# Skip rows in one 512-wide operation, weight loads tied to exps, and a later bank preload in a fused SSM and attention kernel

## Chip, cores and metric

The kernel runs on one core of a Trainium2 chip. The metric is the device time of one execution in microseconds (us). Each kernel was executed several times, and the kernel before ran beside it on the same chip; medians are quoted.

## The reference, cut to what matters

```python
def reference(A_x, ..., B_wqkv, B_wo, gate_w):           # x is 1 x 2048 x 1024
    x = A_x
    g = sigmoid((x * gate_w).sum(-1, keepdims=True))
    # SSM branch: a recurrence over the 2048 positions, then
    #   a = 2 * Re(h @ C^T) + x * Dskip                    <- "x * Dskip" is the skip row
    a = A_ref(x, Lambda, B, C, log_dt, Dskip)
    # attention branch: 32 heads of 32, softmax(q k^T / sqrt(32)) v, then @ wo
    b = B_ref(x, wqkv, wo)
    return g * a + (1 - g) * b
```

## The kernel before

One stream for every engine computes both branches in 512 periods. ScalarE (ACT) does the exps of the scores, TensorE the matmuls, VectorE (DVE) evictions, the SSM scan, skip rows and some exps, and SyncE (SP) issues nearly all DMAs in order. A scheduler notes reads and writes by token and puts in the semaphore waits. These are the parts that the change and the argument touch.

```python
def ld_xn(self, ch, tq, cb):              # two loads of 128 x 256 for one skip row
    for k in range(2):
        c0 = 512 * cb + 256 * k
        self.dma(lambda e, ...: e.dma_start(self.xn[k], self.x2[..., c0:c0 + 256]), [], [("xn", k)] + over, "ld_xn")

def skip_ops(self, ch, tq, cb):           # Ag[:, 0] = xn * g * Dskip, in two halves
    for k in range(2):
        ... scalar_tensor_tensor(self.Ag[:, 0, 256 * k:256 * (k + 1)], self.xn[k], self.gcol[...], self.drow[...], mult, mult)

# SSM output tile: add the matmuls' sum to the skip row, then store the tile
def evac():
    self.dve(... scalar_tensor_tensor(a, ps[:, 7, :], self.gcol[...], a, mult, add) ..., "evac_c")
    self.dma(lambda e: e.dma_start(self.agd[tile], a), ..., "st_a")     # the next skip row overwrites a

# three weight loads of 256 KB for the group after next
for k, part in enumerate((1, 2, 0)):
    if pg == (58 + 2 * k if g else 24):   # pg is the period within its group of 64
        self.ld_w(g + 2, part)

# the tail
self.pv([(last - 1, q) for q in range(4)])
preload()                                 # four 512-wide matmuls that prepare a bank
pv(0); norm(0)                            # last value sums, first part, and their scaling
pv(1); xp(0); norm(1)
```

Every stream ends alike. A check on the results leaves a flag; each engine reads it and jumps over a fallback program to its last block (cut):

```python
def stream(name, e):
    S.emit(name, e, sems, MARK_AT[name], lambda: loc.append(e.mark_branch_hint_location()))
    ...
    e.wait_ge(sems[fast.flag_op.lane], fast.flag_op.tick)
    e.reg_load(r, flag[0:1, 0:1])
    br = e.br_cmp(r, 0, on_true="done_" + name, on_false="bad_" + name, comp_op="IS_EQ")
    br.branch_hint(loc[0])
    with e.bass.body("bad_" + name):      # fallback: 246 instructions on SyncE
        ...
    e.bass.switch_bb("done_" + name)
    if name == "sp":
        S.final_waits(e, sems, True)      # the last stores
```

## Time and profile before

| | before |
|---|---|
| time, median of 3 runs | 918.78 us |
| span of the profiled execution | 916.8 us |
| busy: TensorE, ACT, VectorE | 902.4, 902.1, 757.3 us |
| period of the one visible stall in the body | 2.83 us (others 1.8 to 1.9) |
| flag copy, and the span's end after the start of it | 914.08, 2.8 us later |

Times in a profile count from the start of the profiled execution. The body is bound by ACT (busy 902.1 of 916.8 us, and the weight loads of the score matmuls wait 82.9 us for its exps); the tail from the last exp at 909.59 on is a chain of single steps. The lines of the profile stand in the prediction.

### The profile page before, as it was taken

To read this page: it belongs to the slowest core of one execution; us is meant where nothing else is said; L and a number is where in the kernel's file an instruction comes from. 1 tells how busy PE (TensorE), PEld (TensorE's weight loads), DVE (VectorE), ACT (ScalarE), POOL (GpSimd) and SP (SyncE) were. 2 spreads that over 40 slices of the span, in tenths; PEclk is the share of its full clock that TensorE was granted. 3 is DMA by queue.
4 is the path that set the end of the run, shared out by engine and by line. 5 is a ranking of instruction groups with operands and counts; after the bars stand their busy time and mean duration, and the time that the engine had idled before them with its cause. 6 is when DMAs were issued, how large, how long until landed. Compare 5 with 4: busy or idle time off the path is not lost.

```text
span 916.8 us, 33709 instructions
## 1 busy us (share of the span) xinstructions
PE 902.4 (98%) x15196; PEld 513.6 (56%) x15196; DVE 757.3 (83%) x1394; ACT 902.1 (98%) x1034; POOL 33.4 (4%) x63
## 2 busy tenths in 40 slices
PE   8999999999999999999999999999999999999997
PEld 4556655555555655665556555556555655555554
DVE  4499998999989899998988975789999776676675
ACT  6999999999999999999999999999999999999997
POOL 0500000010000001000000010000000000000000
PEclk9999999999999999999999999999999999999999
DMA  9558631322311305222222113231330122533422
GB/s 205 108 88 129 105 59 40 54 44 57 87 39 39 72 24 86 44 51 48 62 65 31 49 62 87 66 63 31 54 63 8 52 65 70 177 88 119 123 65 75
DMA packets 166867, 65.37 MB, mean 71 GB/s; under 512 B 146880, under 2 KB 155584, under 8 KB 166720
## 3 DMA queue, kind: packets, MB, share of 16 engines
q1 hardware_dynamic: 164416, 62.52, 30.8%
q8 instruction: 120, 1.97, 0.9%
q10 hardware_dynamic: 2304, 0.67, 0.3%
q14 instruction: 27, 0.22, 0.1%
HBM read 21.24 MB, written 12.62 MB: 37 GB/s over the span
## 4 chain that ended last, share of the span: by engine, by line
PE 92%; DVE 3%; ACT 3%; DMA 1%; issue 0%; SPq 0%
PE f_ps L1853 26%; PE f_ps L1758 18%; PE f_ps L1545 12%; PE f_ps L1517 12%; PE f_ps L1485 11%; PE f_ps L1578 6%; PE f_ps L1505 5%; ACT f_cT_re L1781 1%; DVE f_tq L1423 1%; ACT f_pt L1781 1%; DMA f_xT<-in_A_x_dram 1%; ACT f_cT_im L1781 1%; ACT f_Et L1781 1%; ACT f_OT L1781 1%; DVE f_ht L1431 1%
## 5 line engine op out<-in xcount | busy, mean ns | idle before, releaser
L1781 ACT ACTIVATE f_pt<-f_ps 128x1024 bf16<-128x1024 f32 x840 | 800.5, 1156 | 1.2 <-PE f_ps L1758 0.6
L1853 PEld LDWEIGHTS f_ps<-f_V,f_pt 128*128 128x128 bf16 x6720 | 232.8, 96 | 137.1 <-issue 86.5
L1853 PE MATMUL f_ps<-f_V,f_pt 128*128 128x33 bf16 x6720 | 285.4, 178 | 0.3
L1758 PE MATMUL f_ps<-f_Q,f_K 32*128 32x256 bf16 x4096 | 213.1, 273 | 2.6 <-ACT f_cT_re L1781 1.2
L1758 PEld LDWEIGHTS f_ps<-f_Q,f_K 32*128 32x128 bf16 x4096 | 67.4, 92 | 120.9 <-ACT f_pt L1781 63.4
L1517 PE MATMUL f_ps<-f_xT,f_wb 128*128 128x512 bf16 x512 | 131.1, 377 | 1.5 <-DVE f_ub L1523 0.4
L1485 PE MATMUL f_ps<-f_xT,f_wb 128*128 128x512 bf16 x464 | 119.0, 378 | 0.3 <-DVE f_Q L1490 0.2
L1431 DVE TENSOR_TENSOR_SCAN f_ht<-f_pf,f_init,f_ut 128x512 bf16<-128x512 f32 x64 | 81.2, 1275 | 0.0
L1805 DVE TENSOR_SCALAR f_wb<-f_ps 128x512 f32<-128x512 f32 x83 | 56.8, 685 | 27.4 <-PE f_ps L1758 26.5
L1545 PE MATMUL f_ps<-f_cT_re,f_hp 128*128 128x512 bf16 x192 | 72.6, 378 | 0.9 <-DVE f_Ag L1554 0.8
L1545 PE MATMUL f_ps<-f_cT_im,f_hp 128*128 128x512 bf16 x192 | 72.5, 378 | 0.0
L1578 PE MATMUL f_ps<-f_wb,f_OT 128*128 128x512 bf16 x248 | 63.9, 378 | 0.2
L1804 ACT ACTIVATE f_wb<-f_ps 128x512 bf16<-128x512 f32 x83 | 60.8, 732 | 0.6 <-PE f_ps L1758 0.6
L1517 PEld LDWEIGHTS f_ps<-f_xT,f_wb 128*128 128x128 bf16 x512 | 40.3, 96 | 34.2 <-issue 2.2
L1505 PE MATMUL f_ps<-f_wb,f_xT 128*128 128x128 bf16 x896 | 59.1, 219 | 0.3
L1812 DVE SCALAR_TENSOR_TENSOR f_wb<-f_Ag,f_wb 128x512 int16<-128x512 f32 x83 | 56.7, 683 | 0.6
L1811 DVE SCALAR_TENSOR_TENSOR f_Ag<-f_wb,f_Ag 128x512 f32<-128x512 uint16 x83 | 56.7, 683 | 0.5
L1810 DVE SCALAR_TENSOR_TENSOR f_Ag<-f_wb 128x512 f32<-128x512 uint16 x83 | 56.6, 682 | 0.3
L1485 PEld LDWEIGHTS f_ps<-f_xT,f_wb 128*128 128x128 bf16 x464 | 36.2, 96 | 28.7 <-DVE f_Q L1490 0.3
L1505 PEld LDWEIGHTS f_ps<-f_wb,f_xT 128*128 128x128 bf16 x896 | 50.5, 97 | 0.9 <-issue 0.4
L1523 DVE CAST f_ub<-f_ps 128x512 bf16<-128x512 f32 x48 | 33.1, 690 | 14.8 <-PE f_ps L1517 14.1
L1423 DVE TENSOR_TENSOR f_tq<-f_ht,f_Et 128x1024 bf16<-128x1024 bf16 x64 | 42.8, 685 | 0.4
(158 smaller groups left out, 892.7 us busy)
## 6 DMA issues: line engine op xcount, KB each, us to landing
ag_scratch<-f_Ag SPq DMA_DIRECT2D x32, 256.0 KB, 2.0
f_hp<-ag_scratch SPq DMA_DIRECT2D x32, 256.0 KB, 3.0
f_wb<-in_B_wqkv_dram SPq DMA_DIRECT2D x21, 256.0 KB, 4.0
out_dram<-f_xT SPq DMA_DIRECT2D x14, 256.0 KB, 2.1
f_xa<-in_A_x_dram SPq DMA_DIRECT2D x32, 64.0 KB, 1.9
f_pf<-in_A_x_dram SPq DMA_DIRECT2D x32, 64.0 KB, 1.9
f_wb<-in_B_wo_dram SPq DMA_DIRECT2D x1, 1024.0 KB
f_OT<-f_On SPq DMA_TRANSPOSE x63, 2.3
```

The source lines that it names most:

```text
L1431: ops.append((1.192, lambda ri=ri: dve(lambda e: e.tensor_tensor_scan(ht[:, ri, :], rr, ut[:, ri, :], self.init[:, ri, j:j + 1], ALU.mult, ...
L1485: mms.append((1, lambda e, f, l, a=a: e.matmul(ps[:, bank, :], w[:, g % 2, part, a, :], xT[:, a, 512 * ch:512 * (ch + 1)], start=f, stop=l ...
L1505: m = e.matmul(ps[:, bank, 128 * q:128 * (q + 1)], xT[:, a, 128 * kt:128 * (kt + 1)], w[:, g % 2, 2, a, :], start=(a == 0), stop=(a == 7))
L1517: mms.append((1, lambda e, f, l, a=a: e.matmul(ps[:, 7, :], bT[:, n % 2, ri, a, :], xT[:, a, 512 * ch:512 * (ch + 1)], start=f, stop=l), [ ...
L1545: mms.append((1, lambda e, f, l, j=j, ri=ri: e.matmul(ps[:, 7, :], hp(tq, ri, j), cT[ri][:, j, 512 * cb:512 * (cb + 1)], start=f, stop=l), ...
L1578: mms.append((1, lambda e, f, l, j=j: e.matmul(ps[:, 7, :], OT[:, j, 256 * qb + 128 * r:256 * qb + 128 * (r + 1)], wo[j][0][:, 512 * cb:51 ...
L1758: m = e.matmul(ps[:, 2 * sl[z] + h % 2, 256 * kl:256 * (kl + 1)], K[32 * h:32 * h + 32, g % 2, 128 * kt:128 * (kt + 1)], Q[32 * h:32 * h + ...
L1781: self.act(lambda e: e.activation(self.tile[p], ps[:, 2 * s:2 * s + 2, :], ACT.Exp, bias=OCTAVES * LN2, scale=LN2 / 128), [("S", s)], [("p ...
L1804: self.S.op("act", lambda e: e.activation(t[:, 0, :], ps[:, 2 * s, :], ACT.Exp, bias=OCTAVES * LN2, scale=LN2 / 128), reads=[("S", s)], wr ...
L1805: self.S.op("dve", lambda e: e.tensor_scalar(xi, ps[:, 2 * s + 1, :], BITS_0, BITS_MIN, ALU.add, ALU.max), reads=[("S", s)], writes=[("xi" ...
L1811: (0.603, lambda: self.dve(lambda e: e.scalar_tensor_tensor(xw, lo, CUBE_C, xw, ALU.add, ALU.mult), [I, W], [W], "exp_c")),
L1853: m = e.matmul(ps[:, 6, o:o + 33], self.tile[p][:, h2, 256 * kl + 128 * qt:256 * kl + 128 * (qt + 1)], V[:, g % 2, 2 * i + kl, h, :], star ...
```

## The change

Its intent: halve the number of skip-row instructions and loads, space the three weight loads so that they don't crowd a store, and let the last bank preload fill a time in which TensorE waits. The diff, cut to its core (the buffers of the skip rows are joined to match; three runs of the dense order move):

```diff
-DVB_RUNS = (... (502, 506))
+DVB_RUNS = (... (502, 506), (509, 509))          # one more exp half on VectorE
 ...
     def act(self, fn, r, w, name=""):
-        return self.S.op("act", ...)
+        self.last_act = self.S.op("act", ...)
+        return self.last_act
 ...
     def ld_w(self, g, part, eng="sp"):
-        deps = []
+        deps = [self.last_act] if g > 1 else []
 ...
-        for k in range(2):                           # ld_xn
-            self.dma(... self.xn[k] <- 256 columns ...)
+        self.dma(... self.xn <- 512 columns ...)
 ...
-            ops.append((0.335, ... 256 columns ...)) # skip_ops, twice
+        ops = [(0.665, ... 512 columns ...)]
 ...
         self.pv([(last - 1, q) for q in range(4)])
-        preload()
         pv(0)
         norm(0)
+        preload()
         pv(1)
 ...
-    MARK_AT = dict(pe=100, act=260, dve=115, sp=900)
+    MARK_AT = dict(pe=100, act=260, dve=279, sp=900)
```

The last line moves the place of VectorE's branch hint.

## The prediction

> **What bounds the kernel now.** The kernel computes a state-space branch (SSM) and a 32-head attention branch in one stream of 512 periods. Each period does one block of scores on TensorE, two exps of 128x1024 scores on ScalarE (ACT), the value sums (PV) of an older block, and about four 512-wide "dense" matmuls (projections, SSM, output). In 102 of the periods half of one exp goes to VectorE (DVE) as four 512-wide instructions. I read the page first, then the groups by line, then the table of waits, then the timeline.

> ```profile
> PE 902.4 (98%) x15196; PEld 513.6 (56%) x15196; DVE 757.3 (83%) x1394; ACT 902.1 (98%) x1034; POOL 33.4 (4%) x63
> L1781 ACT ACTIVATE f_pt<-f_ps 128x1024 bf16<-128x1024 f32 x840 | 800.5, 1156 | 1.2 <-PE f_ps L1758 0.6
> ```

> Two engines show 98%. The table of waits says which of them waits for the other:

> ```profile
> PEld f_ps L1758 <- ACT f_pt L1781: 63.4, 152, 0.4
> PEld f_ps L1758 <- ACT f_wb L1804: 19.5, 46, 0.4
> DVE f_Ag L1366 <- DMA ag_scratch<-f_Ag: 1.9, 3, 1.0
> PEld f_ps L1545 <- DVE f_Ag L1554: 0.9, 1, 0.9
> ACT f_pt L1781 <- PE f_ps L1758: 0.6, 1, 0.6
> ```

> The weight loads of the score matmuls wait about 83 us for exps in the first two rows, because a bank of scores is free only when an exp has read it. ACT hardly waits for TensorE. So ACT is the bound. Its floor: one run of nine full exps starts at 883.68 and the next exp at 891.91, so a full exp costs 8.23 / 9 = 0.914 us; half exps start about 0.48 us before their successor. The groups have 922 full and 102 half exps: 922 x 0.914 + 102 x 0.48 = 892 us. The first exp starts at 9.77 and the last ends at 909.59, 900 us. Everything that better order can win between is thus about 8 us, 0.9% of the time; behind it lies a tail of 7.2 us.

> The third and fourth wait rows are the one visible stall in the body. In the timeline (start, length, what):

> ```profile
> 566.36 0.57 SPq L1100 DMA_DIRECT2D f_wb<-in_B_wqkv_dram  x1
> ...
> 568.07 0.43 SPq L1555 DMA_DIRECT2D ag_scratch<-f_Ag  x1
> 568.54 1.24 SPq L1100 DMA_DIRECT2D f_wb<-in_B_wqkv_dram  x2
> ...
> 572.47 0.48 DVE L1366 SCALAR_TENSOR_TENSOR f_Ag<-f_xa,f_gcol,f_drow 128x256 f32<-128x256 bf16 x1 [1.02 <-DMA ag_scratch<-f_Ag]
> ...
> 574.47 0.74 DVE L1554 SCALAR_TENSOR_TENSOR f_Ag<-f_ps,f_gcol,f_Ag 128x512 f32<-128x512 f32 x1
> ...
> 575.26 0.10 PEld L1545 LDWEIGHTS f_ps<-f_cT_re,f_hp 128*128 128x128 bf16 x1 [0.95 <-DVE f_Ag L1554]
> ...
> 576.89 0.60 ACT L1804 ACTIVATE f_wb<-f_ps 128x512 bf16<-128x512 f32 x1 [0.62 <-PE f_ps L1758]
> ```

> Read downward: three weight loads (256 KB each) are issued at 566.36 and 568.54, around the store of an SSM row. The store, usually landing in 2.0 us, lands only about 4.4 us after its issue, because the next skip row, which overwrites its source, starts at 572.47. The eviction of the SSM sum slips to 574.47, TensorE waits for the bank until 575.26, and ACT runs dry before 576.89. That period takes 2.83 us from score load to score load, where those without a VectorE exp usually take 1.8 to 1.9.

> [...] with a per-partition scalar, 128, 256 and 512 elements take 342, 477 and 750 ns here, so the fixed part is about 205 ns. [...]

> **The change part by part.**

> *Skip rows.* Now two operations and two 64 KB loads per row, 32 rows:

> ```profile
> L1366 DVE SCALAR_TENSOR_TENSOR f_Ag<-f_xa,f_gcol,f_drow 128x256 f32<-128x256 bf16 x32 | 15.3, 477 | 2.0 <-DMA ag_scratch<-f_Ag 1.9
> L1366 DVE SCALAR_TENSOR_TENSOR f_Ag<-f_pf,f_gcol,f_drow 128x256 f32<-128x256 bf16 x32 | 15.3, 477 | 0.0
> ```

> One 512-wide operation should take about 0.75 us (the 512-wide eviction with the same kind of scalar takes 750 ns). Summed: 32 x (2 x 0.477 - 0.75) = 6.5 us of busy time, or, since two adjacent ones start 0.40 apart and end 0.88 after the first start, 32 x 0.13 = 4.2 us of VectorE time. VectorE is 83% busy and not the bound, so nearly all of this is beside ACT. I give it 0.2 us for rows in which VectorE is late. The 32 saved loads sit on the sync queue, which waits for most of its time anyway: 0.

> *Weight loads tied to exps.* A group's three loads now wait for the latest exp of periods 58, 60 and 62 of the group before. Two periods are about 3.6 us, so by the period starts the loads at the stall should go at about 566.4 (as now), 569.2 and 572.8 instead of 566.4, 568.5 and 569.1. The store then competes with the second half of one load and the first part of another; my estimate for its landing is 2.5 to 3.3 us, that is 570.6 to 571.4. The skip row was ready at 572.47 - 1.02 = 571.45. The wait goes. The period falls from 2.83 to about 1.85: up to 0.98 us. ACT's own loss confirms the size: its exp of 574.97 should be followed at 575.88 by the one of 576.89, 1.0 us. I count 0.9. The two other waits on stores in the third row (0.7 and 0.2) cost ACT nothing visible. The weights are needed only from the next group on, over 3 us later, so lateness of the third is harmless.

> *Order of the rows.* The dense order moves three projections and SSM sums near period 250 and one near period 30. Matmul counts are unchanged. No stall stands there in the waits: 0.

> *One more VectorE exp, in period 509.* This is in the diff, not in its heading. ACT saves 0.914 - 0.48 = 0.43 us. But in the last periods TensorE and VectorE set the pace: each "rest" output row waits for the eviction of the one before.

> *Value sums ahead of the preload.* Now the chain ends so:

> ```profile
> 908.43 0.76 PE L1853 MATMUL f_ps<-f_V,f_pt 128*128 128x33 bf16 x24
> 909.04 1.02 PE L2162 MATMUL f_ps<-f_Et,f_ident 128*128 128x512 bf16 x4
> 909.90 0.36 PE L2173 MATMUL f_ps<-f_V,f_pt 128*128 128x33 bf16 x8
> 910.29 0.18 DVE L2180 RECIPROCAL f_rc<-f_ps 128x4 f32<-128x4 f32 x1 [0.91 <-PE f_ps L2173]
> 911.02 0.35 PE L2173 MATMUL f_ps<-f_V,f_pt 128*128 128x33 bf16 x8 [0.76 <-DVE f_On L2181]
> ```

> The preload (0.87 us on the chain) stands ahead of the value sums, and TensorE then idles 0.76 us behind them for the normalisation. Swapped, the preload fills that idle time: alone it would win about 0.8 us.

> Both together, in the order of the changed instruction streams: VectorE has evict, exp a (period 509), evict, exp b, exp c, evict, exp d, evict; TensorE has, behind the last scores, the eight value sums that need exp d, then a rest row, 32 value sums, the preload. From the present times: second eviction at 905.18, b 905.85, c 906.57, third eviction 907.24, d 907.91 to 908.6 (spacings of 0.67, dependent ones 0.72). TensorE stands from about 907.1 to 908.65 for exp d. Then 0.1 + 3 x 0.216 + 32 x 0.025 brings it to 910.2, and the reciprocal starts 0.19 later, 910.4 against 910.29. So the new VectorE exp eats what the preload wins: tail +0.1 us.

> *Sum.* -0.9 - 0.2 + 0.1 = -1.0 us; I add -0.2 for smaller DMA collisions at the other groups' loads. 918.8 - 1.2 = 917.6.

> **The rivals.** (1) The stall stays or moves: the store is still between two loads, or the third load now delays another transfer. For it: two periods are barely one load's 4.0 us to landing. Against: the skip row has 1 us less to bridge. Then the time is about 918.7. (2) The exp in period 509 is quicker than I reckon, or its value sums do not hold TensorE: then the 0.8 us of the preload is won in full, and 0.1 more from ACT: about 916.6. (3) VectorE's lower load lets its exps finish sooner all over the body. At most it wins part of the 8 us; for it speaks that VectorE is over 90% busy in many slices, against it that TensorE's waits for VectorE are near 1 us in sum outside the stall and normalisations. That would give about 916.

> **Range and chances.** The three known terms are each below 1 us and the three timed runs spread by 0.7 us. Rival 2 or 3 gives the low end 916.1, rival 1 with a worse tail the high end 918.8. 2% is 18 us, over twice what all order could win, and no part adds work on ACT; a failure of another kind keeps 0.01 each.

> **What will show it.** Skip rows of about 750 ns, x32. No wait of a skip row for a store near 572, no 0.95 wait of the SSM matmuls for its eviction, and a period of about 1.85 there. In the tail, a TensorE wait of over 1 us for the last VectorE exp step, and the preload between the two groups of last value sums with hardly any idle time. Were the tail 0.7 us shorter, my timing of exp d is wrong; were the body more than 2 us shorter, ACT had hidden gaps that I did not see.

## The result, and the profile after

The changed kernel took 921.58 us (median of 5 runs, 921.0 to 922.81), the kernel before 918.88 us beside it (5 runs, 918.45 to 919.49). The ratio is 1.0029, 95% interval 1.0015 to 1.0044. (A ratio is the mean time of one kernel's runs over that of the other's in the same rounds, so it is not quite the ratio of the medians.) The prediction was a gain of 1.2 us; it is a loss of 2.7 us, outside the range. All outputs are right.

The bound has not moved. From the page of the changed kernel, busy times and the costliest group:

```profile
PE 882.3 (96%) x14977; PEld 513.4 (56%) x15196; DVE 756.2 (82%) x1366; ACT 902.0 (98%) x1034; POOL 33.4 (4%) x63
L1777 ACT ACTIVATE f_pt<-f_ps 128x1024 bf16<-128x1024 f32 x839 | 799.6, 1155 | 1.3 <-PE f_ps L1754 0.6
```

ACT is as busy as before. TensorE's lower figure is no gain: the page has 14977 matmuls to 15196 weight loads, so 219 matmul records are missing from this trace.

The groups by line show the skip rows as predicted, and with them a first bad sign, the waits in the last column:

```profile
L1362 DVE SCALAR_TENSOR_TENSOR f_Ag<-f_pfx,f_gcol,f_drow 128x512 f32<-128x512 bf16 x32 | 23.9, 746 | 3.8 <-DMA ag_scratch<-f_Ag 3.6
```

They take 746 ns each, but they wait 3.6 us for stores, where the two halves waited 1.9. The timeline of the stall (start, length, what):

```profile
566.62 0.58 SPq L1101 DMA_DIRECT2D f_wb<-in_B_wqkv_dram  x1
...
567.86 0.43 SPq L1551 DMA_DIRECT2D ag_scratch<-f_Ag  x1
...
569.66 3.62 SPq L1101 DMA_DIRECT2D f_wb<-in_B_wqkv_dram  x2
...
572.95 0.75 DVE L1362 SCALAR_TENSOR_TENSOR f_Ag<-f_pfx,f_gcol,f_drow 128x512 f32<-128x512 bf16 x1 [1.23 <-DMA ag_scratch<-f_Ag]
...
575.74 0.10 PEld L1541 LDWEIGHTS f_ps<-f_cT_re,f_hp 128*128 128x128 bf16 x1 [1.16 <-DVE f_Ag L1550]
```

The loads are spaced as foreseen: 566.62, 569.66 and, as the second of the "x2", 572.90. The store between the first two nevertheless lands only 5.0 us after its issue (the view of that one transfer gives its landing), just before the skip row starts. The stall is all there, and the period is 3.04 us long.

The tail of the changed kernel, in the timeline:

```profile
909.21 0.17 PEld L1849 LDWEIGHTS f_ps<-f_V,f_ub 128*128 128x128 bf16 x4 [1.32 <-DVE f_ub L1808]
...
910.58 0.35 PE L2169 MATMUL f_ps<-f_V,f_pt 128*128 128x33 bf16 x8
...
910.97 0.18 DVE L2176 RECIPROCAL f_rc<-f_ps 128x4 f32<-128x4 f32 x1
910.99 0.81 PE L2158 MATMUL f_ps<-f_Et,f_ident 128*128 128x512 bf16 x3
...
911.69 0.35 PE L2169 MATMUL f_ps<-f_V,f_pt 128*128 128x33 bf16 x8
...
914.76 0.14 DVE L2227 CAST flag<-f_ps 1x1 int32<-1x1 f32 x1
```

TensorE waits 1.32 us for the last VectorE exp step, and the preload (910.99; one of its four matmul records is missing) fills the time between the two groups of value sums. The flag copy comes at 914.76, 0.68 us later than before; the body brought 0.64 of that to the tail. So the body and the tail explain only a quarter of the 2.7 us. The rest comes after the flag. The view by windows shows it (window, length, busy time and count of PE, PEld, DVE, ACT, POOL, then granted clock, DMA share, GB/s). First before, then after:

```profile
916.00:917.00 1.00, 0.00 (x0) 0.00 (x0) 0.00 (x0) 0.00 (x0) 0.00 (x0) 0.54 0.16 41
```

```profile
918.00:919.00 1.00, 0.00 (x0) 0.00 (x0) 0.00 (x0) 0.00 (x0) 0.00 (x0) 0.50 0.00 0
919.00:920.00 1.00, 0.00 (x0) 0.00 (x0) 0.00 (x0) 0.00 (x0) 0.00 (x0) 0.50 0.03 8
```

Before, the span ends at 916.8, inside the first line. After, there is a whole microsecond in which no engine works and nothing moves, and in the next one a few KB move. (The granted clock of the changed kernel is 1.00 in the stretches up to 915 us, 0.89 from 915 to 916 and 0.50 from there to the end; over the span that makes its mean of 0.998.) What the engines do there is not in the views, because branches and semaphore instructions aren't counted as work, but the trace has their records. I read SyncE's last ones and the instruction fetches of 8 KB from them:

```
start of                       before    after
flag copy (VectorE)            914.08    914.76
SyncE reads the flag           914.98    916.00
SyncE's branch                 915.76    916.55
SyncE's next instruction       916.29    918.98
8 KB instruction fetches       916.22    916.68
after the flag                 916.49    916.97
                               916.85    917.18
                                         919.55
end of the span                916.84    919.54
```

The next instruction of TensorE, ACT and VectorE follows their branch by 0.49 to 0.61 us before and by 0.49 to 0.62 us after. SyncE's takes 0.53 us before and 2.43 us after, and there is a fourth fetch. The flag to the end takes 2.8 us before and 4.8 us after. That is 2.0 of the 2.7 us.

### The profile page after: what moved, and what is told of

It is laid out like the page before. It is cut to its first block, busy times and chain, and to the rows that moved or that the text cites. A ratio compares the mean times of both kernels' runs of the same rounds, so it can differ in the third digit from the quotient of the medians.

```text
span 919.5 us, 33420 instructions
## 1 busy us (share of the span) xinstructions
PE 882.3 (96%) x14977; PEld 513.4 (56%) x15196; DVE 756.2 (82%) x1366; ACT 902.0 (98%) x1034; POOL 33.4 (4%) x63
## 4 chain that ended last, share of the span: by engine, by line
PE 80%; ACT 11%; DVE 4%; issue 2%; DMA 2%; SPq 1%; DVEq 0%
PE f_ps L1849 23%; PE f_ps L1754 16%; PE f_ps L1541 11%; PE f_ps L1513 11%; PE f_ps L1481 9%; ACT f_pt L1777 7%; PE f_ps L1501 5%; PE f_ps L1574 4%; DMA ag_scratch<-f_Ag 1%; SPq L1093 1%; ACT f_Et L1777 1%; ACT f_cT_re L1777 1%; DMA f_xT<-in_A_x_dram 1%; ACT f_OT L1777 1%; ACT f_cT_im L1777 1%
## 5 line engine op out<-in xcount | busy, mean ns | idle before, releaser
L1513 PE MATMUL f_ps<-f_xT,f_wb 128*128 128x512 bf16 x448 | 118.4, 377 | 8.5 <-issue 3.2
L1481 PE MATMUL f_ps<-f_xT,f_wb 128*128 128x512 bf16 x406 | 106.8, 378 | 5.6 <-issue 1.1
L1427 DVE TENSOR_TENSOR_SCAN f_ht<-f_pfx,f_init,f_ut 128x512 bf16<-128x512 f32 x64 | 81.2, 1274 | 0.0
L1541 PE MATMUL f_ps<-f_cT_im,f_hp 128*128 128x512 bf16 x180 | 68.0, 378 | 3.6 <-DVE f_Ag L1550 1.3
L1541 PE MATMUL f_ps<-f_cT_re,f_hp 128*128 128x512 bf16 x157 | 59.4, 378 | 0.8
L1574 PE MATMUL f_ps<-f_wb,f_OT 128*128 128x512 bf16 x217 | 57.5, 378 | 2.7 <-issue 0.3
```

The lines of the kernel that those rows point to most:

```text
L1427: ops.append((1.192, lambda ri=ri: dve(lambda e: e.tensor_tensor_scan(ht[:, ri, :], rr, ut[:, ri, :], self.init[:, ri, j:j + 1], ALU.mult, ...
L1481: mms.append((1, lambda e, f, l, a=a: e.matmul(ps[:, bank, :], w[:, g % 2, part, a, :], xT[:, a, 512 * ch:512 * (ch + 1)], start=f, stop=l ...
L1513: mms.append((1, lambda e, f, l, a=a: e.matmul(ps[:, 7, :], bT[:, n % 2, ri, a, :], xT[:, a, 512 * ch:512 * (ch + 1)], start=f, stop=l), [ ...
L1541: mms.append((1, lambda e, f, l, j=j, ri=ri: e.matmul(ps[:, 7, :], hp(tq, ri, j), cT[ri][:, j, 512 * cb:512 * (cb + 1)], start=f, stop=l), ...
L1574: mms.append((1, lambda e, f, l, j=j: e.matmul(ps[:, 7, :], OT[:, j, 256 * qb + 128 * r:256 * qb + 128 * (r + 1)], wo[j][0][:, 512 * cb:51 ...
```

## The experiments

Eighteen kernels ran in five batches, each beside the kernel before, whose medians were 918.62, 918.89, 918.68, 918.69 and 918.75 us. "Same" and similar words compare with those.

### The branch hint

The changed kernel with VectorE's hint back at 115, and the kernel before with it at 279. Theory H puts the late end down to the hint's new place.

```diff
-    MARK_AT = dict(pe=100, act=260, dve=279, sp=900)
+    MARK_AT = dict(pe=100, act=260, dve=115, sp=900)     # after_hint115; before_hint279 the other way
```

> The changed kernel with one number put back: VectorE's prefetch hint for the last branch stands again 115 instructions before the end of its stream instead of 279. Theory H[...]: the gap from VectorE's flag copy to the end of the span falls from 4.7 us to about 2.7 us, the fetch on the instruction queue 2.4 us behind the others vanishes, and the time is about 919.6 us. Rival S (the longer end is the landing of the last output stores, made later by the order of the tail): the gap stays 4.7 us and the time stays 921.6 us.

Measured: 921.17 us, ratio 1.0029 (1.0015 to 1.0042), with 2.51 us between SyncE's branch and its next instruction.

> The kernel before with only VectorE's prefetch hint moved from 115 to 279 instructions before the end. Theory H: the gap from the flag copy to the end grows from 2.6 to about 4.7 us and the time rises by 2.0 us to about 920.9 us. Rival S (last stores): no change, 918.9 us. A third reading, that the hint's best place depends on the instruction count of the changed kernel, also gives no change here.

Measured: 918.90 us, ratio 1.0005 (0.9991 to 1.0019), 0.53 us. The place of VectorE's hint changes nothing that these two runs can resolve.

A late hint for SyncE itself was tried later, on the changed kernel:

```diff
-    MARK_AT = dict(pe=100, act=260, dve=279, sp=900)
+    MARK_AT = dict(pe=100, act=260, dve=279, sp=60)
```

> The changed kernel with SyncE's branch hint 60 operations before its end instead of at the start of its stream. If [...]SyncE's own hint comes so early that its effect is gone by the end in the changed kernel: gap 2.8 us, time 919.3. If the hint does nothing for this branch (as the place of VectorE's did nothing for the time): gap 4.8 us, 921.3.

Measured: 921.51 us, ratio 1.0027 (1.0013 to 1.0040), 1.96 us after the branch. That doesn't mend it either.

### Where SyncE's last branch stands

The 32 loads that the change saves, and fewer waits, make SyncE's stream 40 instructions shorter. Counted in the compiled programs, its last branch stands at instruction 378 before and at 338 after; the target at 624 and 584, behind the 246 instructions of the fallback. I put instructions that do nothing back into the middle of SyncE's stream.

```diff
             if mark is not None and k == max(0, n - mark_at):
                 mark()
+            if eng_name == "sp" and pad is not None and k == 100:
+                for _ in range(40):                       # before_pad88_main: 88
+                    eng.nop().then_inc(pad, 1)            # nobody waits for it
```

> The changed kernel with 40 instructions that do nothing (they add one to a semaphore that nobody waits for) put in the middle of SyncE's stream, where it idles; so its last branch and the final block that it jumps to stand at the same places in SyncE's stream (instructions 378 and 624) as in the kernel before. Theory F (the 2.0 us at the end come from where SyncE's last branch and its target stand in the stream, 40 instructions earlier in the changed kernel[...]): the gap from the start of the flag copy to the end of the span falls from 4.8 to 2.8 us, SyncE's next instruction comes 0.45 us after its branch and not 2.35, no fetch after the flag beyond three, time 919.3 (-2.0 or so). Rival G (the late end comes from something in the data traffic or the semaphores of the changed kernel, for example fewer loads counted on the queue): the gap stays 4.8 us and the time 921.3.

Measured: 919.04 us, ratio 1.0002 (0.9989 to 1.0016). SyncE's next instruction comes 0.53 us after its branch, there are three fetches after the flag, and the span ends 2.8 us after the flag copy. This is theory F's outcome (0.53 us for the 0.45 that it expected, 919.04 for 919.3); 40 instructions of no use make the changed kernel 2.1 to 2.5 us faster.

```diff
                     if name == "sp":
                         S2.final_waits(e, sems2)
+                        for _ in range(40):               # in the fallback, never executed
+                            e.nop().then_inc(pad, 1)
```

> The changed kernel with 39 more instructions in SyncE's fallback code, which never runs and which SyncE's last branch jumps over: the branch stays where the change put it (338), its target moves from 584 to 623, the distance grows from 246 to 285. Theory F in its form 'the place of the target counts' (before: 624, 0.45 us): the gap falls to 2.8 us and the time to 919.3. Theory F in its form 'the place of the branch, or the distance, counts': the gap stays 4.8 us, the time 921.3. Rival G: stays, too; the run with 40 in the executed stream tells those two apart.

Measured: 921.10 us, ratio 1.0030 (1.0017 to 1.0044), 2.10 us after the branch, four fetches. The 40 lines add 39 instructions, so the target stands at 623, one short of its old place. Bringing only the target back doesn't help.

> The kernel before with 88 such instructions in the middle of SyncE's stream: its branch stands at 466 and the target at 712, which is 128[...] beyond the places of the changed kernel, so the same place within a fetched block. Theory F with blocks of 128: the kernel before gets the late end: gap 4.8 us, SyncE's next instruction 2.35 us after its branch, one more fetch, time 920.6 (+2.0). With blocks of 256 instead, or under rival G: gap 2.8 us and 918.7, unless the padding itself costs, which it should not, since SyncE is idle there.

Measured: 924.15 us, ratio 1.0055 (1.0042 to 1.0069). The late end came, as F says: 2.42 us after the branch, four fetches, 4.8 us from the flag to the end. But the flag was late as well, at 917.24. The trace has SyncE's 88 extra instructions from 279.76 to 285.29, and the load of a skip row behind them goes out at 285.37, where in the kernel before it went at 280.38; from 300 us on all is 3.1 us late. My assumption that SyncE was idle there was wrong for 88; later runs spread the padding over as many operations.

This run shows one thing more. The padding starts 0.06 us apart, but once there are 0.40 us between two of them: between the 208th and the 209th instruction of SyncE's stream (284.51 and 284.92), and an 8 KB fetch follows at 285.55. I call such a place an edge. Two more show below by a pause of 0.39 us, behind the 336th and the 464th instruction, so the three are 128 instructions apart. I call the 128 instructions from one edge to the next a block.

With spread padding I asked how wide the good range is, and whether it repeats (a step, in the last expectation, is the 128 instructions from one edge to the next):

```diff
+            if eng_name == "sp" and pad is not None and 100 <= k < 122:   # 22, 52; from 80 on: 92, 168
+                eng.nop().then_inc(pad, 1)
```

> The changed kernel with 22 instructions that do nothing spread over SyncE's stream: branch at 360, target at 606, halfway between the slow place (338) and the fast one (378). If only a narrow range of places is fast[...]: slow, SyncE's next instruction 2.3 us after its branch, 921.3. If the range is wide: 0.5 us, 919.3.

Measured: 919.22 us, 0.53 us after the branch.

> The changed kernel with 52 such instructions: branch at 390, target at 636, 12 beyond the fast place. Narrow range of about 10 places: slow, 2.3 us, 921.3. Wide range: 0.5 us, 919.3.

Measured: 918.43 us, 0.53 us.

> The changed kernel with 168 such instructions, one after each of 168 operations: branch at 506, target at 752, which is 128 beyond the fast place of 378. If the places repeat with the 128 instructions of an 8 KB fetch: 0.5 us, 919.3 (somewhat more if the padding delays a transfer). If they repeat with 256 or not at all: 2.3 us, 921.3.

Measured: 919.13 us, 0.53 us.

> The changed kernel with 92 instructions that do nothing, one after each of 92 operations of SyncE: branch at 430, target at 676. [...] If the good range reaches from some place between 341 and 360 to half a step further: slow, SyncE's next instruction 2.3 us after its branch, 921.2. If most places are good and only those around 338 to 350 are bad: 0.5 us, 919.2.

Measured: 919.10 us, 0.53 us. The narrow good range that I had in mind fell: 360, 390, 430 and 506 are as good as 378, and the changed kernel met a bad place. All profiled runs, by the place of the branch, with the time from SyncE's branch to its next instruction and the number of 8 KB fetches after the flag:

```
branch at               runs                                                    us          fetches
338                     after, after_hint115, after_no509, after_sp_hint_late   1.96-2.51   4
338 (target at 623)     after_pad40_fallback                                    2.10        4
340                     after_loads_late                                        2.31        4
466 (= 338 + 128)       before_pad88_main                                       2.42        4
360                     after_pad22                                             0.53        3
378                     before, before_hint279, before_swap, before_skip,
                        after_pad40_main, best_a, best_b                        0.53        3
379, 380                before_tie, best_c                                      0.53        3
390, 430                after_pad52, after_pad92                                0.53        3
506 (= 378 + 128)       after_pad168                                            0.53        3
```

No run falls between the two kinds, and the edges sort them. In every slow run the branch is the second or the fourth instruction behind an edge (337 and 465 are the first). The pause of 0.39 us shows there, too: just ahead of the read of the flag in the runs at 338 and 466, and two instructions earlier in the run at 340. Here are SyncE's last records of three runs (W a wait, R the read of the flag, B the branch, N the next instruction):

```
kernel changed, 338:    W 915.54  W 915.61  R 916.00  B 916.55                       N 918.98
loads late, 340:        W 914.69  W 915.08  W 915.17  R 915.24  B 915.76             N 918.07
before, 378:            W 914.86  W 914.92  R 914.98  B 915.76                       N 916.29
```

So in the slow runs SyncE passes an edge, and its branch starts 0.9 to 1.1 us after the last instruction ahead of that edge. In the fast ones the last edge is at least 23 instructions back. The fourth fetch after the flag fits: above, a fetch came 0.6 us behind the 209th instruction, the first after an edge, and in the slow runs such a fetch would fall behind the flag. (The last fetch of a run is not the extra one: in all profiles, fast and slow, it comes 0.55 to 0.81 us after SyncE's next instruction.) How near the target is does not sort the runs. Counted on in steps of 128, which no pause shows for the targets, the slow branch at 338 has its target (584) in the next block and all fast ones in the next but one; but after_pad40_fallback, with its target there as well, is slow (2.10 us).

### The spacing of the weight loads

First the tie alone, on the kernel before.

```diff
-        deps = []
+        deps = [self.last_act] if g > 1 else []
```

> The kernel before with only the tie of the weight loads to the exp activations. As I predicted for this part: the stall near 572 us is gone, -0.9 us, 917.8. As the changed kernel's trace has it: the loads are spaced (3 us apart) but the stall stays, 2.8 to 3.0 us for period 321, time 918.7 to 919.0. Its SyncE stream is one instruction longer (branch at 379 instead of 378): if that alone moves it over an edge the end gap is 4.8 us and the time 2.0 more; I expect 2.8 us.

Measured: 918.75 us, ratio 1.0001 (0.9988 to 1.0015). The timeline:

```profile
566.21 0.57 SPq L1101 DMA_DIRECT2D f_wb<-in_B_wqkv_dram  x1
...
567.93 0.43 SPq L1556 DMA_DIRECT2D ag_scratch<-f_Ag  x1
569.25 3.62 SPq L1101 DMA_DIRECT2D f_wb<-in_B_wqkv_dram  x2
...
572.62 0.48 DVE L1367 SCALAR_TENSOR_TENSOR f_Ag<-f_xa,f_gcol,f_drow 128x256 f32<-128x256 bf16 x1 [1.31 <-DMA ag_scratch<-f_Ag]
```

The tie spaces the loads and removes nothing. Then I moved the loads of the changed kernel so that none is issued just ahead of that store.

```diff
-                    if pg == (58 + 2 * k if g else 24):
+                    if pg == ((60, 62, 63)[k] if g else 24):
```

> The changed kernel with the hint at 115 and the three weight loads of a group issued in periods 60, 62 and 63 instead of 58, 60 and 62, so that in the group before period 320 none stands ahead of the store of an SSM row in the queue. Theory Q (a store waits behind the weight load issued just before it, not for those issued after it): the store near 568 us lands in 2 to 3 us instead of 5.0, the skip row's wait of 1.2 us and TensorE's wait of 1.2 us vanish, that period takes about 1.85 us instead of 3.04, and the time is 1.0 to 1.2 us below the changed kernel with the hint at 115. Rival B (any weight load in flight slows the store, whichever comes first): the store still lands in over 4 us and the time does not move.

Measured: 919.71 us, ratio 1.0013 (0.9999 to 1.0026), the late end included (it has the hint at 115, so its neighbour is the 921.17 of after_hint115). The timeline:

```profile
567.50 0.33 SPq L1551 DMA_DIRECT2D ag_scratch<-f_Ag  x1
569.49 3.62 SPq L1101 DMA_DIRECT2D f_wb<-in_B_wqkv_dram  x2
...
571.46 0.74 DVE L1362 SCALAR_TENSOR_TENSOR f_Ag<-f_pfx,f_gcol,f_drow 128x512 f32<-128x512 bf16 x1
...
574.98 0.58 SPq L1551 DMA_DIRECT2D ag_scratch<-f_Ag  x1
...
578.36 0.75 DVE L1362 SCALAR_TENSOR_TENSOR f_Ag<-f_pfx,f_gcol,f_drow 128x512 f32<-128x512 bf16 x1 [0.88 <-DMA ag_scratch<-f_Ag]
```

The first store has no load ahead of it, and two behind it, the first of them 2 us later: its skip row doesn't wait, and the period is 1.90 us. The next store is issued 0.4 us behind the third load, and there the wait comes back, 0.88 us, in a period of 2.41. So taking away the load just ahead of the store was enough here to end this wait, from 1.23 us to none.

It is not all that delays a store, though. The first store landed 3.4 us after its issue, between the 2 to 3 us of theory Q and the over 4 us of rival B, where most stores take 2.0. In the changed kernel the store issued at 764.11, with no weight load within 4 us of it, took 4.0 us by its landing record, and its skip row waited 1.06 us. The one at 777.88, with the load of the output weights 0.4 us behind it and none ahead, took 4.4 us, and its skip row waited:

```profile
777.88 0.33 SPq L1551 DMA_DIRECT2D ag_scratch<-f_Ag  x1
778.25 0.43 SPq L2006 DMA_DIRECT2D f_wb<-in_B_wo_dram  x1
782.43 0.75 DVE L1362 SCALAR_TENSOR_TENSOR f_Ag<-f_pfx,f_gcol,f_drow 128x512 f32<-128x512 bf16 x1 [0.51 <-DMA ag_scratch<-f_Ag]
```

What else makes a store late is not shown here. The profiled body gained only about 0.3 us at the flag (913.99 for 914.27), less than the 1.5 us between the medians; the intervals of both are about a microsecond wide to each side.

### The exp of period 509 and the preload

```diff
-DVB_RUNS = (... (502, 506), (509, 509))
+DVB_RUNS = (... (502, 506))
```

> The changed kernel with the hint back at 115 and without the VectorE exp in period 509 (it is a ScalarE exp again); the value sums stay ahead of the preload. By the prediction's reckoning of the tail the 1.2 us wait of TensorE for the last VectorE exp step goes and the preload's gain shows: 0.7 to 0.9 us less than the changed kernel with the hint at 115, about 918.8 us. Rival (the reordered value sums win nothing by themselves, the wait only moves): within 0.2 us of it.

Measured: 919.80 us, ratio 1.0017 (1.0003 to 1.0030), against 921.17 with it. The flag copy comes at 913.48 instead of 914.27, 0.8 us earlier; most of the rest of the spans' difference (917.9 for 919.1) is the late end, which happens to be 2.03 us here and 2.51 there. Then the preload alone, on the kernel before:

```diff
         self.pv([(last - 1, q) for q in range(4)])
-        preload()
         pv(0)
         norm(0)
+        preload()
         pv(1)
```

> The kernel before with only the bank preload moved behind the value sums of the last block's first part and its scaling; no exp of period 509 on VectorE, everything else as before. As predicted for this part alone: the reciprocal of the tail comes 0.8 us earlier, the preload fills the wait between the two groups of value sums, time 918.0 (-0.8). If something else ends the tail (the preload now in the way of the second group): 918.7.

Measured: 917.76 us, ratio 0.9990 (0.9978 to 1.0003), 0.9 us less than 918.69. The timeline of its tail:

```profile
909.09 0.35 PE L2173 MATMUL f_ps<-f_V,f_pt 128*128 128x33 bf16 x8
...
909.29 1.02 PE L2162 MATMUL f_ps<-f_Et,f_ident 128*128 128x512 bf16 x4
909.48 0.18 DVE L2180 RECIPROCAL f_rc<-f_ps 128x4 f32<-128x4 f32 x1
...
910.21 0.35 PE L2173 MATMUL f_ps<-f_V,f_pt 128*128 128x33 bf16 x8
```

The reciprocal comes at 909.48 instead of 910.29, 0.8 us earlier, and the preload lies in the former wait. The interval just reaches no gain, but time, reciprocal and flag (913.27 for 914.08) agree.

### The fused skip row alone

The parts of the change for ld_xn, skip_ops and the joined buffer, with the changed dense order (the old order's build refused the fused row), on the kernel before, padded so that the branch stays at 378.

```diff
+        ops = [(0.665, lambda: self.dve(lambda e: e.scalar_tensor_tensor(self.Ag[:, 0, :], self.xn, ...512 columns...)))]
```

> The kernel before with only the fused skip row of the change (one load and one operation of 512 columns, with the order of the fill work that the changed kernel has), and 41 instructions that do nothing spread over SyncE's stream so that its last branch stays at 378. As predicted for this part: 32 operations of 750 ns in place of 64 of 480, beside ScalarE, worth -0.2 us or nothing: 918.5 to 918.9. Rival: the row now needs both halves of the buffer at once, so it waits longer for the store before it (the changed kernel has a wait of 0.5 us at 782 and +0.3 us at the opening): 919.2 to 919.6.

Measured: 919.22 us, ratio 1.0008 (0.9995 to 1.0022): not a gain, perhaps a small loss. The row at the stall waits 1.61 us for its store, and the flag comes at 914.50, 0.4 us later than before:

```profile
567.35 0.43 SPq L1552 DMA_DIRECT2D ag_scratch<-f_Ag  x1
567.82 1.38 SPq L1102 DMA_DIRECT2D f_wb<-in_B_wqkv_dram  x2
...
572.80 0.75 DVE L1363 SCALAR_TENSOR_TENSOR f_Ag<-f_pfx,f_gcol,f_drow 128x512 f32<-128x512 bf16 x1 [1.61 <-DMA ag_scratch<-f_Ag]
```

A wait at this place varies by itself (1.02, 0.97 and 0.63 us in three profiles of kernels with the old loads and rows), so I count the loss as open. One thing does repeat. With one load of the row to issue instead of two, SyncE issues this store 1.2 us behind the first weight load instead of 1.7; it then took 4.5 to 5.5 us to land in the eleven profiles with fused rows and a load ahead of it, and 3.9 to 4.6 us in the five with halves. Counted from the issue of the weight load, the store landed at about the same time, after 5.75 to 6.7 us with fused rows and 5.6 to 6.3 us with halves. So the earlier issue gained nothing here.

### All mended

best_a is the changed kernel without period 509, with the loads in periods 60, 62 and 63 and with padding that puts the branch at 378. best_b moves the loads further, in the one group where they met a store. best_c is the kernel before with the later preload, the tie and the loads as in best_b, and with the skip rows still in two halves.

```diff
-                    if pg == (58 + 2 * k if g else 24):
+                    if pg == (((56, 60, 61) if g == 4 else (60, 62, 63))[k] if g else 24):   # best_b, best_c
-            if p == 437:
+            if p == 438:                                                                     # best_b
```

> The changed kernel without the VectorE exp in period 509, with the three weight loads of a group in periods 60, 62 and 63 instead of 58, 60 and 62, and with 38 instructions that do nothing spread one by one over SyncE's stream, so that its last branch stands at 378 as in the kernel before. If the three causes found so far add up: 921.3 (changed) - 2.0 (branch) - 1.0 to 1.4 (period 509) - 0.3 to 0.5 (store ahead of the loads) = 917.4 to 918.0, which is 0.9 to 1.5 us under the kernel before; end gap 2.8 us. If they overlap or the padding delays a transfer (88 of them in one place delayed one by 3 us): 918.5 or more.

Measured: 917.43 us, ratio 0.9989 (0.9975 to 1.0002). Its trace still has a wait of 0.20 us at the former stall, where the store took 4.1 us with no load ahead of it, and one of 0.83 us behind the third load.

> As best_a, but in the group whose loads met a store the loads stand in periods 56, 60 and 61, so that none of them is issued within 3 us ahead of a store, and the 768 KB load of the output weights starts one period later (438), away from the store behind which it stood. If a store waits for the weight load that is just ahead of it in the queue: neither period 321 nor period 324 shows a wait of the skip row for a store (0 instead of 1.2 and 0.9 us), the wait at 782 us goes too, 0.5 to 1 us less than best_a: 916.6 to 917.3. If not, the same as best_a within 0.3.

Measured: 917.11 us, ratio 0.9983 (0.9969 to 0.9996). The timeline at the former stall has no wait:

```profile
567.63 0.33 SPq L1553 DMA_DIRECT2D ag_scratch<-f_Ag  x1
569.62 2.21 SPq L1103 DMA_DIRECT2D f_wb<-in_B_wqkv_dram  x2
571.60 0.74 DVE L1364 SCALAR_TENSOR_TENSOR f_Ag<-f_pfx,f_gcol,f_drow 128x512 f32<-128x512 bf16 x1
```

The later load of the output weights did not come about: it was still issued 0.4 us behind the store, at 777.22, and the wait at 781 stayed (0.27 us). So nothing follows from that part.

> The kernel before with the later preload and the tie of the weight loads, the loads of the group that met a store in periods 56, 60 and 61 and those of the others in 60, 62 and 63; the skip rows stay two operations of 256 columns each, no exp of period 509 on VectorE, SyncE's last branch at 380. 918.7 (before) - 0.9 (preload) - 0.9 (stall near 572 us, if the skip rows in two halves don't bring another wait there) = 916.9, and 916.5 if the fused row itself cost 0.4 in the version that has it (917.1). If the split rows need the store as late as the fused ones: 917.1. If the loads so placed wait for something else: 917.8.

Measured: 917.11 us, ratio 0.9984 (0.9971 to 0.9998). best_b and best_c beat both kernels, by 1.6 us against the one before. They are alike, so the fused row is worth nothing here that these runs can resolve (they differ in the dense order and the padding as well).

## Why the prediction was wrong

The bound was right: ACT is busy for the same 902 us, and nothing in the change touched it.

**"The wait goes ... I count 0.9"** failed. The step that failed is the landing of the store: 2.5 to 3.3 us were estimated for it once the loads are spaced, between the usual 2.0 and the 4.4 seen with the loads around it. With all three loads spaced by 3.0 and 3.2 us it took 5.0 us (4.6 with the tie alone), and the stall stayed (1.23 us of wait, and 1.31 with the tie alone). The first load, 1.2 to 1.7 us ahead of the store, was still there; with none just ahead the wait was 0 in three kernels and 0.20 us in best_a. The prediction's rival 1 had this outcome, at 918.7, and before_tie measured 918.75. The size of the stall fits what its removal brings, but isn't resolved: best_c, without it, is 0.65 us below before_swap, and their intervals are over a microsecond wide to each side.

**"nearly all of this is beside ACT. I give it 0.2 us"** was right in its mechanism: 746 ns each, x32, and no time gained. But the 0.2 did not come: alone the part measured 919.22 against 918.68, with an interval that includes no change, and best_b and best_c show no difference.

**"the new VectorE exp eats what the preload wins: tail +0.1 us"** was right. From entering the tail to the flag the changed kernel takes 0.04 us more. The step's own parts were measured too: the preload alone won 0.9 us (predicted 0.8), and taking out the exp gave 0.8 us back.

**"The 32 saved loads sit on the sync queue, which waits for most of its time anyway: 0"** is the step that cost most. SyncE's waits do sum to 751 of the 916.8 us before, and as transfers the loads show no gain: before_skip, without them and with the branch still at 378, measured 919.22 against 918.68. But leaving out instructions moved SyncE's last branch from 378 to 338, and from there the jump over the fallback took 2.43 us instead of 0.53. The padding that restores the places restores the time (919.04). The sum of the prediction's steps had no entry for what follows the flag. With that end mended the padded versions take 918.4 to 919.2 us, about as long as the kernel before: the rest of the change comes to nothing, because the stall stays and the two changes in the tail cancel.

So a taken branch can cost far more than usual here (1.96 to 2.51 us for 0.53). The target's distance does not decide: at the same distance of 246 instructions the branch was slow at 338, 340 and 466, and fast at seven other places. What the runs show is that a branch two or four instructions behind an edge was slow, and one 24 or more behind it was not. What the branch waits for is not shown: the slow runs have one 8 KB fetch more after the flag (four for three), but the queue doesn't say for which engine a fetch is, and no run put the branch between the 4th and the 24th place. Every branch here carries a hint, and no run left it out, so why the fast ones are fast is open too.

One reading of the prediction was a little off, without effect on its sum: its run of nine exps begins with a step of 0.98 us. The other eight take 0.906 us each, so the floor is about 884 us and not 892, and better order could win some 16 us and not 8.

Also open are the 0.64 us by which this one profile of the changed kernel entered the tail later: about 0.2 are the longer stall and 0.4 a second wait for a store at 782 us, but other profiles of the same body have their flag anywhere from 913.94 to 914.91, and the late-hint run even at 916.50 with an ordinary median time.

## What to carry to other kernels

When a change shortens an instruction stream that ends in a jump, look at the records behind the last useful instruction: a taken branch can cost 2 us or not, by where it stands in the stream (2.43 us at 338 and 0.53 at 378 here), and some instructions that do nothing can move it to a better place (40 of them brought 921.58 us to 919.04); spread them, since 88 in one place made the later work 3.1 us late. To protect a store that something waits for, keep big loads from being issued just ahead of it on the same queue (the wait of 1.23 us here was gone without one), and check its landing in the trace: spacing the loads among themselves did not help here (a wait of 1.31 us with the tie alone), and a load 0.4 us behind a store came with a late landing too (4.4 us, where most took 2.0). And two improvements that fill the same wait, like the preload and the extra exp in the tail, must be measured one by one, since together they can show nothing (0.9 us won and 0.8 given back here).
